# A chunked linear-attention and expert kernel on one core: scaling of group 0 read from the SBUF table, and a new order of all steps

## The chip, the core and the metric

The kernel runs on one core of a Trainium2 chip. Its engines work at the same time, each through its own instructions strictly in the order in which they were written: TensorE (PE in the profile, with PEld for its weight loads), VectorE (DVE), ScalarE (ACT), GpSimd (POOL) and SyncE (SP), which here only issues transfers. An instruction that waits holds up everything behind it on its engine. The metric is the device time of one execution in microseconds (us); lower is better.

## The reference

The first part is a linear attention with decay, for 4 batches, 8 heads, 768 time steps and head size 48. Its output `y`, as a matrix `x` of 3072 tokens by 384, goes through a two-layer block with a smooth ReLU between the layers.

```python
for t in range(S):
    cur = np.einsum('bhd,bhe->bhde', u[None] * kt, vt)
    y[:, :, t] = np.einsum('bhd,bhde->bhe', rt, state + cur)
    state = w[None, :, :, None] * state + np.einsum('bhd,bhe->bhde', kt, vt)
h = x @ w_in                      # 384 -> 2048
g = np.where(h >= 1, h, np.where(h <= -1, 0, (h + 1) ** 2 / 4))
out = g @ w_out                   # 2048 -> 384
```

Inputs and output are float32; the kernel computes its matrix products in bfloat16.

## The kernel before

The 768 steps are cut into 6 chunks of 128, and the 4 batches into 2 pairs; a pair's chunk is a *group*, so there are 12 groups, 0 to 11, of two units (batches) each. Groups 2c and 2c+1 are chunk c. A unit n has 128 tokens, one per partition. Inside a chunk the decay is taken out by scaling R up with w to the power t-64 (table Wup) and K down with its inverse (table Wdn).

Steps of a group g, by their names in the code; a suffix `.0` or `.1` means one unit alone:

- `LR`, `LK`, `LV` (line 252) load R, K and V on SP's queue, 384 KB each or 192 KB for a unit; `WI0` to `WI2` (line 243) and `WO0`, `WO1` (line 246) load the two weight matrices on GpSimd's queue, as bfloat16. `WI0` serves quarter 0 of the hidden layer, `WI1` quarter 1, `WI2` quarters 2 and 3.
- `Rs`, `Ks`, `KU`, `RKU` (line 271) are the products R·Wup, K·Wdn, K·u, R·K·u. `us` (line 293) sums the last over a head, `V` casts V to bfloat16 on ScalarE, `B` (line 302) is V times that sum.
- Rs and Ks have to stand transposed. Groups 0 and 1 and 2 do that on TensorE (`TR`, `TK`, `T`, line 319) and copy it out of PSUM (`cR`, `cK`, `c`); from group 3 on it is a DMA transpose on SP's queue (`RT`, `KT`, line 307).
- `A` (line 359; `AA` for both units) are the 128x128 products of K and R by head; `AT` (lines 368, 373) masks them on VectorE; `Y` (lines 421, 427) multiplies by V and by the state; `y` or `yg` (lines 435, 439) adds B. `Sp`, `Tm`, `decayg`, `sbf` carry the state on.
- The tokens are transposed to xT, by TensorE (`X`, `xc`) for the first groups and by a DMA transpose on SP's queue (`xcg`, line 456) from group 3 on.
- `m g.q` (line 464) is quarter q of the first layer: 12 matmuls of 256 columns into PSUM (`hp`). ScalarE squares the clamped value (`r`, lines 472 and 475; `s`, lines 482 and 484), VectorE ends it (`g`, line 487). `M g.jq` (line 499) is unit j and quarter q of the second layer, 4 matmuls of 384 columns into `op`. `og` or `o` copies it to SBUF, `stg` or `st` (lines 518, 515) stores it.
- `Z n` (line 526) is n matmuls on a zero tile, whose result nobody reads.

The order of all of this is one written-out list, `ORDER`; a loop at the end of the function calls the steps word by word, so each engine's and each queue's own order follows from the list. `=V`, `=A`, `=G` choose VectorE, ScalarE or GpSimd, and the digits behind a slash choose PSUM banks. Tiles come from pools with a fixed number of buffers (`SLOTS`), and a step that takes a buffer waits until the last reader of the old tile is done: for output tiles `o` that is the landing of the store.

In the preamble the logarithm of w is broadcast to all partitions by a matmul with ones (`bw`, line 206, tile `lwp`), and ScalarE takes exponentials of it: into SBUF (`WupS`, `WdnS`, lines 221 and 224), and into two PSUM banks (`Wup`, `Wdn`, lines 214 and 218, tiles `up_t` and `dn_t`), which only the `Rs` and `Ks` of group 0 read:

```python
t = flat(Wup) if g else tiles["up_t"]
```

Of the kernel before, what the change touches and what calls it, by code (L numbers as in the profile page):

```python
# [34 lines left out]
M1.01 AA3/13 AT6 X4/0 xc4=A M1.02 X5/0 xc5=A M1.03 og1=A LK5 AT7 Y6/1 m2.0/0 sbf3=A us3 Rs4=G RT4 Sp4/2 Sp5 Tmg2
r2.0=A s2.0=A B3=G Y7 yg3 xcg3 m2.1/3 r2.1=A m2.3/2 LV4 m2.2/1 Ks4=G KT4 g2.0 M2.00/0 M2.10 s2.1=A g2.1 M2.01 M2.11
LV6 r2.2=V m3.1/3 stg0 KU4=G RKU4=G LK6 LR6 r2.3=A s2.3=A s2.2=A decayg2=G g2.3 r3.1 m3.0/2 g2.2 M2.02 M2.03 Sp6/1 Sp7
us4 s3.1=A KU5=G M2.12 Ks5=G r3.0 g3.1 M2.13 s3.0=A KT5 Tmg3 og2=A Rs5=G m3.2/3 g3.0 LV5 V4 AA4/01 AT8 sbfg2=A
decayg3=G m3.3/2 RT5 AT9 B4=G M3.00/0 stg1 r3.2 s3.2=A M3.01 Y8/1 Y9 RKU5=G r3.3 g3.2 yg4 xcg4 s3.3=A V6 M3.10 M3.02
g3.3 KU6=G V5 sbfg3=A M3.11 LK10 stg2 us5 M3.12 M3.03 LR7 AA5/21 AT10 M3.13 Rs6=G og3=A m4.0/3 AT11 B5=G r4.0 LK7  # L40
m4.1/2 s4.0=A Y10/0 Y11 m4.2/1 r4.1 s4.1=A yg5 Ks6=G xcg5 RKU6=G m4.3/0 g4.0 RT6 M4.00/3 M4.10 r4.2 s4.2=A g4.1 Rs7=G
M4.11 Sp8/2 Sp9 KT6 M4.01 g4.2 LV7 LR8 M4.02 m5.1/1 LR9 r4.3 Tmg4 s4.3=A g4.3 decayg4=G us6 B6=G r5.1 KU7=G AA6/02
AT12 M4.03 LK8 sbfg4=A AT13 M4.12 M4.13 m5.0/0 s5.1=A RT7 g5.1 Ks7=G og4=A Y12/2 Y13 m5.2/1 r5.0 s5.0=A m5.3/3 yg6
xcg6 g5.0 RKU7=G Sp10/2 Sp11 r5.2 s5.2=A M5.00/0 M5.10 Ks8=G KT7 Tmg5 M5.11 LK9 decayg5=G g5.2 M5.01 M5.02 us7 m6.1/2
r5.3 s5.3=A g5.3 stg3 V7 LR11 B7=G r6.1 AA7/13 AT14 M5.12 KU8=G KT8 sbfg5=A s6.1=A M5.13 AT15 Rs8=G M5.03 og5=A m6.0/1
g6.1 LV8 r6.0 KU9=G RT8 s6.0=A Rs9=G Y14/3 Y15 Sp12/0 yg7 m6.2/2 m6.3/3 Sp13 xcg7 r6.2 stg4 g6.0 M6.00/1 s6.2=A Tmg6
decayg6=G r6.3 RT9 g6.2 M6.10 RKU8=G LR10 M6.11 Ks9=G M6.01 s6.3=A g6.3 stg5 M6.12 m7.1/0 AA8/32 M6.02 V8 r7.1 AT17
s7.1=A M6.13 KT9 M6.03 AT16 m7.0/2 sbfg6=A Sp14/3 Sp15 LV10 KU10=G us8 B8=G og6=A stg6 g7.1 r7.0 m7.2/1 s7.0=A Tmg7
LV9 Rs11=G g7.0 Y16/0 Y17 decayg7=G m7.3/3 yg8 r7.2 s7.2=A M7.00/2 xcg8 M7.10 Ks10=G r7.3 g7.2 s7.3=A g7.3 M7.11 M7.01
M7.02 V10 AA9/01 AT18 RT11 RKU9=G V9 M7.12 AT19 KT10 sbfg7=A M7.13 RKU10=G LK11 m8.0/3 Rs10=G M7.03 us9 r8.0 us10  # L50
og7=V s8.0=A g8.0 B9=G m8.1/1 r8.1 Y18/0 Y19 RT10 B10=G s8.1=A yg9 m8.2/2 r8.2 KU11=G xcg9 m8.3/3 s8.2=A g8.1 M8.00/0
LV11 M8.10 r8.3 M8.01 Sp16/1 g8.2 Sp17 Tmg8 M8.11 M8.12 stg7 m9.0/2 s8.3=A decayg8=G g8.3 AA10/31 AT21 M8.13 r9.0
M8.02 AT20 s9.0=A M8.03 m9.1/1 V11 sbfg8=A Y20/3 Y21 g9.0 Ks11=G og8=A yg10 xcg10 m9.2/0 r9.1 KT11 s9.1=A M9.00/3 r9.2
s9.2=A g9.1 m9.3/2 RKU11=G stg8 g9.2 M9.10 M9.11 r9.3 Sp18/1 Sp19 Tmg9 s9.3=A M9.01 M9.02 g9.3 decayg9=G us11 m10.0/0
r10.0 B11=G AA11/12 M9.12 M9.13 AT23 s10.0=A M9.03 sbfg9=A AT22 og9=V m10.1/2 stg9 Y22/1 Y23 g10.0 m10.2/3 r10.1
M10.00/0 s10.1=A r10.2 yg11 xcg11 g10.1 M10.10 m10.3/1 s10.2=A g10.2 r10.3 s10.3=A M10.01 M10.11 m11.1/2 M10.12 M10.02
g10.3 r11.1 m11.0/3 s11.1=A g11.1 M10.13 m11.2/1 r11.0 m11.3/2 s11.0=A r11.2 s11.2=A g11.0 M10.03 M11.10/3 og10=V
M11.11 r11.3 stg10 g11.2 M11.00/0 M11.01 M11.02 s11.3=A g11.3 M11.12 M11.13 M11.03 o11.1=A st11.1 o11.0=A st11.0
# [15 lines left out]
def kernel(  # L74
# [193 lines left out]
    def product(e, out, a, b, g, j):  # L268
        j0, j1 = by_unit(g, j)
        part = lambda x: x.rearrange("p (b h) d -> p b h d", b=UNITS)[:, j0:j1]  # L270
        engines[e].tensor_mul(part(out)[:, :, :, :D], part(a), rep(b, j1 - j0) if len(b.shape) == 3 and b.shape[1] == H else part(b))  # L271
# [295 lines left out]
```

## Time and profile before

| | |
|---|---|
| Median of 3 runs | 178.05 us (178.02 to 178.56) |
| The profiled execution's own time | 177.88 us |
| Its span, first to last instruction | 176.1 us |
| TensorE busy | 163.8 us, 93% of the span |
| VectorE, ScalarE, GpSimd busy | 131.0, 129.3, 114.9 us |
| Moved by DMA | 28.78 MB in 105,703 packets, of which 100,946 are under 512 bytes |

The span leaves out 1.78 us of the execution's time that lie ahead of its first and behind its last profiled instruction. The shares of busy time are means over a load-heavy first part, a long middle, and a tail; they don't say what ends a wait in any one of them. R, K and V are read in rows of 48 floats, 192 bytes, hence the small packets. `q1` is the transfer queue that SP issues to, `q0` that of GpSimd.

### The profile page before, as it was taken

How to read it: one execution, taken by the hardware profiler on the slowest of the kernel's cores; microseconds unless marked ns; L12 is line 12 of the kernel's file. 1: busy time of each engine (PE TensorE's matmuls, PEld its weight loads, DVE VectorE, ACT ScalarE, POOL GpSimd, SP SyncE). 2: the span in 40 equal slices, each digit the busy share in tenths (PEclk: the TensorE clock that was granted, in tenths of full speed). 3: DMA queues.
4: the chain of work that ended last, by engine and by line, in shares of the span. 5: the costliest groups of instructions: out<-in, count | busy, mean ns of one | idle time of the engine just before them, and what ended most of it. 6: DMA issues, size and time to landing. Idle time of an engine off the chain costs nothing.

```text
span 176.1 us, 3979 instructions
## 1 busy us (share of the span) xinstructions
PE 163.8 (93%) x1638; PEld 129.0 (73%) x1638; DVE 131.0 (74%) x149; ACT 129.3 (73%) x150; POOL 114.9 (65%) x83
## 2 busy tenths in 40 slices
...
GB/s 113 196 183 189 202 184 190 207 204 195 160 187 161 177 262 153 240 266 163 174 204 168 179 254 176 217 263 231 183 111 178 45 48 149 4 134 2 2 90 92
DMA packets 105703, 28.78 MB, mean 163 GB/s; under 512 B 100946, under 2 KB 104788, under 8 KB 105684
## 3 DMA queue, kind: packets, MB, share of 16 engines
...
q0 software_dynamic: 1744, 3.15, 9.8%
q8 instruction: 13, 0.21, 0.6%
...
q10 hardware_dynamic: 4, 0.00, 0.0%
HBM read 20.45 MB, written 4.72 MB: 143 GB/s over the span
## 4 chain that ended last, share of the span: by engine, by line
PE 51%; DMA 20%; SPq 15%; ACT 4%; DVE 4%; issue 2%; POOL 1%; ACTq 0%; POOLq 0%
PE hp L464 25%; PE op L499 20%; SPq L252 14%; DMA Ri<-in_r_dram 8%; DMA out_dram<-o 8%; DMA RT<-Rs 2%; DVE g L487 2%; DMA xT<-y 2%; PE A L359 2%; ACT pt L475 2%; PE Y L427 2%; PE Y L421 1%; ACT sq L484 1%; PE Sp L394 1%; POOL Rs L271 1%
## 5 line engine op out<-in xcount | busy, mean ns | idle before, releaser
L487 DVE SCALAR_TENSOR_TENSOR g<-sq,hp 128x1024 bf16<-128x1024 bf16 x48 | 58.4, 1218 | 17.1 <-ACT sq L484 16.8
L464 PE MATMUL hp<-xT,w_in 128*128 128x256 bf16 x576 | 68.8, 273 | 1.0 <-DMA xT<-y 0.8
L499 PE MATMUL op<-w_out,g 128*128 128x384 bf16 x384 | 68.5, 326 | 0.2 <-DVE g L487 0.2
L464 PEld LDWEIGHTS <-w_in 128*128 128x128 bf16 x576 | 61.9, 114 | 4.5 <-DMA xT<-y 1.4
L475 ACT ACTIVATE pt<-hp 128x1024 f32<-128x1024 f32 x46 | 46.9, 1019 | 19.1 <-PE hp L464 19.1
L499 PEld LDWEIGHTS <-g 128*128 128x128 bf16 x384 | 35.9, 98 | 22.4 <-DVE g L487 1.2
L484 ACT ACTIVATE sq<-pt 128x1024 bf16<-128x1024 f32 x46 | 48.7, 1058 | 1.4
L368 DVE TENSOR_TENSOR AT<-A,umask 128x1024 bf16<-128x1024 f32 x20 | 23.6, 1220 | 8.2 <-PE A L359 8.0
L271 POOL TENSOR_TENSOR Rs<-Ri,Wup 128x768 bf16<-128x768 f32 (+1 forms) x11 | 19.4, 1760 | 9.7 <-DMA Ri<-in_r_dram 9.7
L271 POOL TENSOR_TENSOR KU<-Ki,u_sb 128x768 f32<-128x768 f32 (+1 forms) x13 | 21.2, 1635 | 4.7 <-ACT u_sb L111 4.7
L271 POOL TENSOR_TENSOR RKU<-Ri,KU 128x768 f32<-128x768 f32 (+1 forms) x13 | 21.2, 1638 | 1.9 <-DVE KU L271 1.7
L405 POOL TENSOR_TENSOR state<-Tm,wCm 128x768 f32<-128x768 f32 x8 | 14.6, 1831 | 11.7 <-DVE Tm L402 11.7
L302 POOL TENSOR_TENSOR V<-Vb,diag 128x768 f32<-128x768 bf16 (+1 forms) x13 | 17.2, 1330 | 5.6 <-ACT Vb L111 4.5
L271 POOL TENSOR_TENSOR Ks<-Ki,Wdn 128x768 bf16<-128x768 f32 (+1 forms) x10 | 17.9, 1786 | 2.2 <-DMA Ki<-in_k_dram 2.1
L439 DVE TENSOR_TENSOR y<-Y,V 128x768 bf16<-128x768 f32 x10 | 9.6, 956 | 5.7 <-POOL RKU L271 2.4
L293 DVE TENSOR_REDUCE diag<-RKU 128x16 f32<-128x768 f32 (+1 forms) x14 | 11.6, 831 | 0.6 <-POOL RKU L271 0.6
L111 ACT COPY o<-op 128x768 f32<-128x768 f32 (+1 forms) x10 | 7.4, 737 | 6.3 <-PE op L499 3.3
L111 ACT CAST Vb<-Vi 128x768 bf16<-128x768 f32 (+1 forms) x14 | 10.2, 736 | 1.5 <-DMA Vi<-in_v_dram 1.5
L427 PE MATMUL Y<-Vb,AT 128*128 128x48 bf16 x192 | 10.5, 185 | 0.6 <-DVE state L398 0.6
L427 PEld LDWEIGHTS <-AT 128*128 128x128 bf16 x192 | 9.3, 97 | 1.4 <-issue 0.8
L402 DVE TENSOR_TENSOR Tm<-Sp,state 128x768 f32<-128x768 f32 x8 | 7.6, 955 | 1.5 <-PE Sp L394 1.4
L111 ACT CAST state_bf<-state 128x768 bf16<-128x768 f32 (+1 forms) x12 | 8.5, 720 | 0.0
...
## 6 DMA issues: line engine op xcount, KB each, us to landing
...
w_out<-in_moe_w_out_dram POOLq DMA_DIRECT2D x2, 768.0 KB, 10.2
...
```

What stands on the lines that cost most here:

```text
L111: nc.scalar.copy(out, in_) if e == "A" else engines[e].tensor_copy(out, in_)
L252: nc.sync.dma_start(out=t[:, j0 * H : j1 * H, :], in_=source(x, g, j0, j1))
L271: engines[e].tensor_mul(part(out)[:, :, :, :D], part(a), rep(b, j1 - j0) if len(b.shape) == 3 and b.shape[1] == H else part(b))
L302: engines[e].tensor_mul(t[:, hs, :], tiles["V", g][:, hs, :], tiles["diag", g][:, hs].unsqueeze(2).to_broadcast([P, n, D]))
L368: nc.vector.tensor_mul(t.rearrange("p i n t -> p (i n) t"), tiles["A", n].rearrange("p i (n t) -> p (i n) t", t=P), umask.unsqueeze(1).to_ ...
L405: engines[e].tensor_mul(states[g % BP], tiles["Tm", g], flat(wCm).unsqueeze(1).to_broadcast([P, UNITS, DM]))
L427: nc.tensor.matmul(Y[:, h * D : (h + 1) * D], AT[:, i, p, :], V[:, j * H + h, :], start=(c == 0), stop=True, skip_group_check=True,)
L464: nc.tensor.matmul(hp[:, f, :], w_in_sb[wi][:, i, wo * FG * P + f : (wo + 1) * FG * P : FG], tiles["xT", g][:, :, i, :], start=(i == 0), s ...
L475: nc.scalar.activation(t, tiles["hp", g, q], AF.Relu, bias=0.5, scale=0.5)
L484: nc.scalar.activation(t, p, AF.Square)
L487: nc.vector.scalar_tensor_tensor(out=make("g", ("g", g, q), [P, FG, TOK], BF16), in0=tiles["sq", g, q], scalar=1.0, in1=tiles["hp", g, q], ...
L499: nc.tensor.matmul(tiles[key][:, k, :DO], tiles["g", g, q][:, f, j * P : (j + 1) * P], w_out_sb[wi][:, wo, f * DO : (f + 1) * DO], start=( ...
```

## The change

Four things are changed.

1. The step `Wup` isn't in the list any more, so there is no PSUM table `up_t`; `Rs` of group 0 reads the SBUF table. (`Wdn` and its PSUM table stay, and `Ks` of group 0 still reads it.) All three steps `Rs0.0`, `Rs0.1`, `Rs1.0` run on VectorE.
2. The whole list is laid out anew: other positions, PSUM banks and, for some steps, other engines. `KU` of groups 0 and 3 and of unit 1.1 and `RKU` of group 1 go to VectorE, `RKU0.1`, `Ks1.1` and `Rs1.1` to GpSimd; the list keeps one step of each kind and unit.
3. There are 97 idle matmuls in the list where there were 56; those ahead of `bw` have 48 columns, the others 128.
4. Output tiles `o` have three buffers instead of two.

The diff, with the list cut to the lines that matter below:

```diff
 ORDER = """
-Zs/0 LK0.0 LR0.0 LK0.1 LR0.1 LR1.0 LR1.1 ln Z19 bw/2 WupS bu/1 Wdn/0 Ks0.1=V Wup/1 uS=A KU0.1=G Ks0.0=V Z5 TK0/3
-Rs0.0=V TR0/1 cK0=V Rs0.1=V TK1/0 cK1=A RKU0.1=V LV0.0 LV0.1 KU0.0=V RKU0.0=G WdnS us0.1 cR0=A Z14 A0/23 us0.0 AT0.0
-TR1/0 cR1=A Z4 A1/01 Rs1.1=V WI0 WI1 LK1.0 LK1.1 V0.0 wq/2 wE B0.0=G Rs1.0=G LV1.0 LV1.1 AT1.0 AT0.1 Z4 Y0/2 WI2 TR3/0
-LK2.0 AT1.1 Ks1.0=G cR3=A Ks1.1=V Z6 TK3/1 cK3=V V0.1 B0.1=G LR2.0 LR2.1 V1.0 y0 TR2/3 cR2=V LK2.1 Z2 A3/01 AT3.0 X0/2
-xc0=V KU1.1=G Y1/3 y1 KU1.0=G RKU1.0=G TK2/0 cK2=V Z2 X1/2 AT3.1 A2/30 AT2.1 wC=A Sp1/1 Tm1 xc1=A m0.0/0 r0.0=A s0.0=A
-m0.1/1 r0.1=A LK3 us1.0 AT2.0 RKU1.1=G us1.1 Sp2/0 Tm2 LR3 Y2/0 V1.1 Sp3/1 s0.1=A B1.0=V Y3/3 y2 X2/2 xc2=A g0.0
-m0.2/0 r0.2=A B1.1=G y3 X3/0 Sp0/2 g0.1 s0.2=A m0.3/1 r0.3=A s0.3=A Tm3 Tm0 xc3=V m1.2/3 m1.0/2 g0.2 WO0 WO1 Rs2=G
...
+Zs/1 LR0.0 LK0.0 LK0.1 ln Z44 bw/2 LR0.1 LR1.0 Wdn/0 bu/1 LV1.0 WupS LV0.0 Ks0.0=V Rs0.0=V uS=A KU0.0=V LV0.1 TK0/3
+cK0=A Ks0.1=V WdnS RKU0.0=G Z8 TR0/3 cR0=A WI0 KU0.1=V Rs0.1=V LK1.0 LK1.1 Z8 A0/12 TK1/0 WI1 TR1/3 AT0.0 cK1=A us0.0
+RKU0.1=G cR1=A V0.1 Z8 A1/13 LR1.1 V0.0 Rs1.0=V AT0.1 B0.0=G AT1.1 Z13 TR2/2 Y0/0 us0.1 wq/3 AT1.0 B0.1=G LV1.1 y0
+Y1/1 wE wC=V cR2=A Ks1.0=G Z2 X0/3 xc0=A y1 Z10 X1/0 KU1.0=G xc1=A TK2/1 cK2=A Z4 m0.0/0 WI2 RKU1.0=V V1.0 us1.0 LK2.0
+Sp1/3 A2/12 r0.0=A Tm1 m0.1/1 KU1.1=V LK2.1 s0.0=A AT2.0 Rs1.1=G Ks1.1=G g0.0 TR3/0 cR3=A AT2.1 r0.1=A TK3/0 B1.0=V
+LR2.0 Y2/3 Sp2/2 cK3=A y2 V1.1 RKU1.1=V A3/10 X2/3 us1.1 xc2=A AT3.1 s0.1=A B1.1=G Sp0/3 AT3.0 Sp3/0 WO0 m0.3/0 LR2.1
+g0.1 WO1 LR3 Y3/1 Tm2 m0.2/1 r0.3=A y3 Tm3 KU2=G LK3 s0.3=A Tm0 Ks2=G r0.2=A X3/1 xc3=V g0.3 m1.1/2 s0.2=A m1.0/3
+LV2.0 r1.1=V g0.2 RKU2=G m1.2/0 s1.1=A m1.3/1 Rs2=G g1.1 r1.2=A s1.2=A M0.00/2 r1.3=V M0.01 r1.0=A s1.3=A M0.10 g1.2
+M0.11 us2 T5/0 s1.0=A M0.12 g1.3 M0.13 c5=A LV2.1 M0.02 g1.0 sbf1=A A5/1 Rs3=G T4/0 AT5 M1.00/3 c4=A LV3 M1.10 sbf3=A
+Ks3=V M1.01 M1.11 A4/1 KU3=V KT3 M1.02 V2 AT4 RT3 M1.12 sbf0=A B2=G Sp4/0 Y4/1 LR4 Y5 Sp5 M0.03 RKU3=G yg2 LK4 M1.03
+og0=A Tmg2 X4/1 LK5 M1.13 xc4=A us3 sbf2=A decayg2=G X5/0 AA3/21 xc5=A m2.0/0 V3 AT6 LV5 og1=A B3=G AT7 m2.1/2 r2.0=A
...
-SLOTS = {..., "g": 13, "o": 2}
+SLOTS = {..., "g": 13, "o": 3}
...
     def do_Rs(e, b, g, j=None):
-        t = flat(Wup) if g else tiles["up_t"]
+        t = tiles["up_t"] if g == 0 and "up_t" in tiles else flat(Wup)
...
     def do_Ks(e, b, g, j=None):
-        t = flat(Wdn) if g else tiles["dn_t"]
+        t = tiles["dn_t"] if g == 0 and "dn_t" in tiles else flat(Wdn)
...
     def do_Z(e, b, n):
+        cols = P if "lwp" in tiles else D
         for i in range(n):
-            nc.tensor.matmul(tiles["z"][:, 0, :P], idle[:, :P], idle[:, :P], start=True, stop=True)
+            nc.tensor.matmul(tiles["z"][:, 0, :cols], idle[:, :P], idle[:, :cols], start=True, stop=True)
```

Further down both lists go through the groups in the same way, m, M, AA and Y of one group beside those of the next. What stands on TensorE's side of the list between a transfer's issue and the step that reads it differs:

| issue to reader | old list | new list |
|---|---|---|
| `xcg3` to `m3.1` | 3 m, 4 M | 1 m, 3 M |
| `RT5` to `AA5` | 7 M, 2 Y | 5 M, 2 Y |
| `xcg5` to `m5.1` | 1 m, 5 M, 2 Sp | 4 M |
| `RT8` to `AA8` | 3 m, 5 M, 2 Y, 2 Sp | 1 m, 5 M, 1 Sp |

Ahead of `M0.00`, counted from `m0.0`, the old list has 8 m, 2 Y, 3 Sp and 2 X on TensorE, the new one 8 m, 2 A, 2 Y, 4 Sp, 2 X, one `TR` and one `TK`; between `M0.00` and `AA3` it is 14 M, 2 T, 2 A, 2 Y in the old one and 16 M, 2 T, 2 A, 2 Y, 2 Sp, 2 X in the new one. The last output steps are `o11.1` and `o11.0`, on VectorE and ScalarE in the new list, both on ScalarE in the old one.

More of the change, by code (lines that the diff above doesn't have):

```diff
@@ L30 @@
-m0.1/1 r0.1=A LK3 us1.0 AT2.0 RKU1.1=G us1.1 Sp2/0 Tm2 LR3 Y2/0 V1.1 Sp3/1 s0.1=A B1.0=V Y3/3 y2 X2/2 xc2=A g0.0
-m0.2/0 r0.2=A B1.1=G y3 X3/0 Sp0/2 g0.1 s0.2=A m0.3/1 r0.3=A s0.3=A Tm3 Tm0 xc3=V m1.2/3 m1.0/2 g0.2 WO0 WO1 Rs2=G
-Ks2=G m1.1/0 r1.2=V g0.3 m1.3/1 KU2=G RKU2=G s1.2=A g1.2 LV2.0 LV2.1 LV3 M0.00/3 M0.10 M0.01 r1.0=A s1.0=A g1.0 r1.3=A
-s1.3=A M0.11 g1.3 M1.00/2 sbf1=A sbf0=A M1.10 Rs3=G M0.12 M0.13 T4/1 r1.1=A s1.1=A M0.02 M0.03 Ks3=V KT3 KU3=G c4=A
-T5/1 c5=A g1.1 us2 V2 B2=G A4/0 AT4 M1.11 RT3 LR4 LK4 A5/1 AT5 og0=A LR5 M1.12 M1.13 Y4/0 Y5 yg2 sbf2=A V3 RKU3=G
@@ L35 @@
[L35 to L58, printed above, removed]
+Zs/1 LR0.0 LK0.0 LK0.1 ln Z44 bw/2 LR0.1 LR1.0 Wdn/0 bu/1 LV1.0 WupS LV0.0 Ks0.0=V Rs0.0=V uS=A KU0.0=V LV0.1 TK0/3
```

25 lines of the change are left out of this document (24 added, 1 removed).

## The prediction

> **What bounds the kernel now.** I read the page first, then the chain of waits, then TensorE's timeline and its waits, then the transfer queues by windows.
>
> ```profile
> span 176.1 us, 3979 instructions
> PE 163.8 (93%) x1638; PEld 129.0 (73%) x1638; DVE 131.0 (74%) x149; ACT 129.3 (73%) x150; POOL 114.9 (65%) x83
> ```
>
> ```profile
> 25.58 14.41 DMA Ri<-in_r_dram
> ...
> 42.59 4.36 DMA RT<-Rs
> ...
> 47.09 0.62 PE A L359 x16
> ...
> 51.22 0.34 PE Sp L394 x8
> ...
> 60.53 4.72 DMA out_dram<-o
> ...
> 157.99 1.30 PE op L499 x8
> ...
> 163.86 2.62 PE hp L464 x24
> ...
> 168.15 4.52 DMA out_dram<-o
> ...
> 172.77 0.48 ACT o L111
> ```
>
> These are pieces of the chain that ended last. Up to 47 us it is SP's queue and the transfers behind it (R of group 3, then its transpose); from there it is nearly all TensorE. One m costs 1.31 us, one M 0.65, an AA 0.6 (so an A 0.3), a Sp 0.17.
>
> ```profile
> 19.90 2.78 PE L464 MATMUL hp<-xT,w_in 128*128 128x256 bf16 x24
> ...
> 24.89 0.33 PE L394 MATMUL Sp<-Vb,Ks 128*128 128x96 bf16 x4 [1.03 <-ACT Vb L111]
> ...
> 34.34 1.95 PE L499 MATMUL op<-w_out,g 128*128 128x384 bf16 x11
> ...
> 66.18 0.62 PE L359 MATMUL A<-RT,KT 48*128 48x128 bf16 x16 [0.83 <-ACT o L111]
> ...
> 68.07 1.46 PE L499 MATMUL op<-w_out,g 128*128 128x384 bf16 x8
> 69.37 0.21 PE L421 MATMUL Y<-state_bf,RT 128*128 128x96 bf16 x1
> ...
> 70.12 3.62 PE L499 MATMUL op<-w_out,g 128*128 128x384 bf16 x20
> ...
> 74.44 0.62 PE L359 MATMUL A<-RT,KT 48*128 48x128 bf16 x16 [0.69 <-DMA RT<-Rs]
> ...
> 166.32 6.01 PE L499 MATMUL op<-w_out,g 128*128 128x384 bf16 x36
> ```
>
> This is TensorE's timeline, with what ended its idle time in brackets. The first hp matmul starts at 19.90, the first op matmul at 34.34, the last ends at 166.32 + 6.01 = 172.33. Two Y take 70.12 - 69.37 = 0.75. So TensorE's own work from the first hp on is 48 x 1.31 + 96 x 0.65 = 125.3 for m and M, and about 18.7 for the rest (9 AA 5.4, 22 Y 7.9, 19 Sp 3.2, some transposes and two A 2.2): 144.0. The stretch is 172.33 - 19.90 = 152.4, so 8.4 us are lost. By stage: up to `M0.00` 14.44 - 11.8 = 2.6; from there to `AA3` at 47.09, 12.75 - 11.4 = 1.35; behind it 125.24 - 120.8 = 4.4. The time is the sum of four terms: the start of the first hp, the work behind it, what is lost, and a tail of 176.1 - 172.3 = 3.8.
>
> ```profile
> q1 hardware_dynamic: 10382, 1.96, 135.5%
> q0 software_dynamic: 1, 0.00, 0.2%
> ...
> q0 software_dynamic: 1189, 1.56, 84.3%
> q1 hardware_dynamic: 2577, 0.49, 31.0%
> ...
> q0 software_dynamic: 535, 1.55, 89.9%
> q1 hardware_dynamic: 1276, 0.24, 16.9%
> ```
>
> These are packets and MB of the two queues: SP's queue q1 alone from 2.8 to 13.0 us; both from 13.0 to 23.5, while w_in comes in; both from 28.4 to 37.5, while w_out does. The sum is 0.19 to 0.20 MB/us in each, a ceiling, but while weights flow q1 has only 0.047 and then 0.026 MB/us of it. Up to the landing of R of group 3 (25.58 + 14.41 = 40.0), ten inputs of 0.393 MB and 3.15 MB of weights have come, 7.1 MB in 37.2 us: the early part is set by bytes.
>
> **The named part: no PSUM table for R.**
>
> ```profile
> 6.13 1.02 DVE L271 TENSOR_TENSOR Ks<-Ki,dn_t 128x384 bf16<-128x384 f32 x2 [3.21 <-ACT dn_t L218]
> ...
> 6.02 0.56 ACT L214 ACTIVATE up_t<-lwp,up_col 128x384 f32<-128x384 f32 x1
> ...
> 7.07 0.55 DVE L271 TENSOR_TENSOR Rs<-Ri,up_t 128x384 bf16<-128x384 f32 x1
> ...
> 11.85 0.55 DVE L271 TENSOR_TENSOR Rs<-Ri,Wup 128x384 bf16<-128x384 f32 x1
> ```
>
> The timelines of VectorE and ScalarE have the product from the PSUM table and from the SBUF table at 0.55 us each: the operand's place costs nothing. ScalarE loses one exponential, 0.56. The new list puts `Wdn` first, so `Ks0.0` starts one exponential earlier, some 0.4 us, and `Rs0.0` finds `WupS` ready behind it. Were it slower instead, each of three 0.55 us products would grow; the nearest row, the same product on GpSimd at 1.0, bounds that at 1.4 us, and the two equal rows speak for 0.
>
> **When the first hp starts.**
>
> ```profile
> 7.07 1.00 POOL L271 TENSOR_TENSOR KU<-Ki,u_sb 128x384 f32<-128x384 f32 x1 [4.71 <-ACT u_sb L111]
> ...
> 10.69 1.70 POOL L243 DMA_DIRECT2D w_in<-in_moe_w_in_dram  x2
> ...
> 14.14 0.80 POOL L243 DMA_DIRECT2D w_in<-in_moe_w_in_dram  x1
> 14.97 1.39 POOL L271 TENSOR_TENSOR Ks<-Ki,Wdn 128x384 bf16<-128x384 f32 x1
> ...
> 25.69 1.48 POOL L246 DMA_DIRECT2D w_out<-in_moe_w_out_dram  x2
> 27.18 1.86 POOL L271 TENSOR_TENSOR Rs<-Ri,Wup 128x768 bf16<-128x768 f32 x1
> ```
>
> GpSimd's timeline. In the new list `KU0.0` is on VectorE, again behind u_sb (7.0), done at 7.55; `RKU0.0` on GpSimd follows until 8.55, and `WI0`, `WI1` are issued at 8.6, 2.1 us earlier. Their packets began 2.3 us behind the issue (10.69; one q0 packet lies ahead of 13.0), so now near 10.9. By then q1 has moved 8.1 x 0.193 = 1.56 MB, eight half loads of 0.197: K, R, V of group 0, R1.0 and V1.0 are in. The ninth, K1.0, still lacks 0.2 MB and gets q1's 0.047 MB/us: it lands near 15.5. The attention chain of group 0 itself, walked by rows (`Y0` 12.4, `y0` 13.3, `X0` 13.9, `y1` 14.4, `X1` 15.0, copy until 15.9), is ready earlier. But `TK2` stands ahead of `m0.0` on TensorE, and it needs `Ks1.0`, 1.39 us on GpSimd: 15.5 + 1.4 + a transpose and four idle matmuls 0.6 gives **17.5** for the first hp. Lower bound, if K1.0 were in before the weights, 16.4 (the copy of `X1`, then the same 0.6); upper bound, if q1 stands still until both weight parts are through (10.9 + 0.786/0.149 = 16.2, then 1 us for the load), 19.2.
>
> That is 2.4 us earlier, but 1.3 us of work that used to lie ahead of `m0.0` (two A, TR, TK, Sp) now lie behind: 145.3 instead of 144.0.
>
> The Trainium skill, DMA: Bandwidth & Descriptors, section Queues, rings and completion order, says that a DMA engine goes round its queues packet by packet. With 1 KB weight packets against 192 bytes, K1.0 would get 0.03 MB/us, land near 16.5 and set the first hp at 18.5, and as the same microsecond runs on through `WI2`, the sum would be 177.0; the measured 2577 packets against 1189 say that q1 gets more than one for one.
>
> **From there to `M0.00`.** `WI2` moves behind `Ks1.0` and `KU1.0` (15.5 + 1.4 + 1.0 = 18.0), 3.9 us later than the 14.14 of before; packets from 20.3, 0.786 MB at 0.15 to 0.18: in at 25.1. `m0.3` waits for it, where unhindered it would come at 17.5 + 4.8 = 22.3. Behind it stand 6 m, Y and X, 8.3 us, so `M0.00` at 33.4; VectorE, with `g` of 1.22 and `r1.1`, `r1.3` also on it, holds `m1.3` back by 0.6. I take **34.0** (33 to 35), against 34.34: most of the early lead is paid back to w_in, since the bytes haven't changed.
>
> **To `AA3`.** R and K of group 3 land by 40 as before, being the same bytes. `Ks3`, on VectorE behind `AT5`, is done near 41.8, and KT3 and RT3 go out after it, landing near 47.5 by the 4.36 of the chain. TensorE has 13.4 us of work in front of `AA3` now: 34.0 + 13.4 = 47.4. So **47.5**, later than 47.09, but with 118.8 us of work left instead of 120.8. The lead there is 120.8 + 47.09 - 118.8 - 47.5 = 1.6 us.
>
> **Behind `AA3`.**
>
> ```profile
> DMA to landing us min/median/max: 2.7/4.8/6.7
> ...
> DMA to landing us min/median/max: 2.8/4.8/6.6
> ...
> DMA to landing us min/median/max: 2.8/2.8/4.1
> ```
>
> ```profile
> 69.51 2.28 SPq L307 DMA_TRANSPOSE RT<-Rs  x1
> ```
>
> Issue to landing of the transposes KT, RT and xT, and SP's issue of `RT5`. The stall of 0.83 (1.0 in all) at 66.18 was `og2` waiting for the store that left at 60.53 to free an `o` buffer; with three buffers it goes. But the list leaves less work between issue and reader: `RT5` to `AA5` 4.0 us instead of 5.3, `xcg5` to `m5.1` 2.6 instead of 4.9, `xcg3` to `m3.1` 3.3 instead of 6.6, `RT8` to `AA8` 4.7 instead of 8.3. SP issued `RT5` 1.4 us behind its place in the list, which is ahead of `M3.00` (68.07), and I take the same lag for the others; against medians of 4.8 and 2.8 that lacks up to 2.2 at RT5, 1.6 at xT5, 0.9 at xT3, 1.5 at RT8. Each stall pushes TensorE back and so eases the next one; I take somewhat over half, 3.5, and 0.8 for small ones: 4.3, as before. GpSimd has one `KU` less there, at nothing on the path.
>
> **The tail.** `o11.0` waited from 172.33 for the store of `og10` (168.15 + 4.52 = 172.67) and started at 172.77. The third buffer frees it: 0.4 us.
>
> **The sum.** 47.5 + 118.8 + 4.3 = 170.6 for the last matmul (172.33 before), tail 3.4: span 174.0. With the 1.78 us between span and execution (177.88 - 176.1) that is 175.8; the median of the runs lies 0.17 above that execution, so **176.0**.
>
> **Rivals.**
>
> *The early lead stays.* If K1.0 and `WI2` don't hold TensorE up more than V1.1 did before (2.6 and 1.35 lost), the end is 16.4 + 145.3 + 7.4 (8.4 less the `o` stall) = 169.1, and the time 174.4. For it: `V1.1`, whose cast ended the 1.03 stall at 24.89, now lands ahead of `WI2`. Against it: the ceiling in MB/us.
>
> *Nothing comes of it.* `AA3` waits for RT3 until 49, because `Ks3` and `KU3` are now queued on VectorE between `AT5` and `AT4`, and the late stalls stay: 1.5 us more, 177.5.
>
> *R of group 2 starves (slower).* `T5` needs `Rs2`, which stands behind `RKU2` on GpSimd, and both need R2.1. By bytes R2.1 is in at 2.8 + (16 x 0.197 + 1.57)/0.193 = 27.3; w_out's packets begin about 27.5 in the new list. If w_out is first, R2.1 lands only at its end (27.5 + 9.1 = 36.6), `RKU2` and `Rs2` (1.86 each) end at 40.3, and `T5`, due at 34.0 + 2.6 = 36.6, holds TensorE for 3.7: 179.7. It decides from R2.1 landing later than 33. In the old kernel `Rs2` ran at 27.18, ahead of w_out.
>
> *The transposes are late one after another (slower).* If the four stalls come at full length and with the longest landings, 6.6 and 4.1, rather than medians, another 3 to 4 us: 179.5.
>
> That removing the PSUM table does nothing by itself is no rival but what the rows say; the sum doesn't rest on it.
>
> **Chances.** Forecast 0.43 (its own range 174.9 to 177.2), lead stays 0.15, nothing 0.18, starving 0.12, late transposes 0.10, anything else slower 0.02. A measurement tells 0.3%, 0.53 us, from no change. Faster: 0.43 + 0.15 and a quarter of the nothing case, less a little of the forecast's upper edge: 0.60. Same: 0.14. Slower: 0.26. The range leaves out the far ends of the slower cases and the best of the lead: 173.6 to 179.4.
>
> **What would show it.** Right: first hp between 16.4 and 19, just behind `TK2`; TensorE waiting for w_in or hp ahead of `m0.3`; `M0.00` within 1 us of 34; `AA3` with X4, X5 and all M1 done ahead of it; no wait of A on `o`; waits of A on RT or of hp on xT between 60 and 115 us. Wrong: `M0.00` ahead of 32.5 (the ceiling on bytes was misjudged), a wait at the transposes of `T5` (starving), or over 6 us lost behind `AA3`.

## The result, and the profile after

The changed kernel takes 180.73 us, the median of 18 executions (178.36 to 183.24), against 178.08 (176.84 to 179.87) for the kernel before on the same chip. The ratio is 1.011, with a 95% interval of 1.008 to 1.014: slower by 1.1%. A ratio here leaves out executions more than 1.5% above the fastest of their kernel, on either side, so it can lie below the quotient of two medians. The prediction was 176.0 with a range of 173.6 to 179.4: wrong, on the other side. The profiled execution of after took 180.69 us.

The page of the changed kernel: its span, TensorE's row, and the granted clock in 40 slices of 4.5 us.

```profile
span 178.9 us, 4053 instructions
PE 165.8 (93%) x1679; PEld 131.1 (73%) x1679; DVE 136.6 (76%) x152; ACT 128.6 (72%) x149; POOL 111.0 (62%) x80
...
PEclk9999987999999999999999996999999999999999
```

The span grew by 2.8 us. By the profile's windows the granted clock was at half twice, from 25.2 to 28.6 and from 107.1 to 110.5 us, and both times TensorE had m steps to run. In the kernel before it was at half once, from 13.1 to 16.5 us, ahead of any m.

TensorE's timeline of after, at the marks that the prediction used:

```profile
17.78 0.92 PE L464 MATMUL hp<-xT,w_in 128*128 128x256 bf16 x7
...
36.32 0.98 PE L499 MATMUL op<-w_out,g 128*128 128x384 bf16 x5
...
50.10 0.62 PE L359 MATMUL A<-RT,KT 48*128 48x128 bf16 x16
...
73.66 0.62 PE L359 MATMUL A<-RT,KT 48*128 48x128 bf16 x16 [0.84 <-DMA RT<-Rs]
...
106.63 4.45 PE L464 MATMUL hp<-xT,w_in 128*128 128x256 bf16 x24 [2.08 <-DVE o L111]
110.91 0.51 PE L394 MATMUL Sp<-Vb,Ks 128*128 128x96 bf16 x8
...
170.12 5.36 PE L499 MATMUL op<-w_out,g 128*128 128x384 bf16 x32
```

| mark on TensorE, us | before | predicted | after |
|---|---|---|---|
| first hp | 19.90 | 17.5 | 17.78 |
| `M0.00` | 34.34 | 34.0 | 36.32 |
| `AA3` | 47.09 | 47.5 | 50.10 |
| last matmul ends | 172.33 | 170.6 | 175.48 |
| tail | 3.8 | 3.4 | 3.4 |

So two stretches hold 4.3 of the 4.9 us by which the last matmul comes too late: from the first hp to `M0.00` 18.5 us instead of 16.5, and behind `AA3` 125.4 instead of 123.1.

Ahead of the first stretch there is a wait. TensorE's, VectorE's and GpSimd's timelines of after, between 13.8 and 17.1 us:

```profile
14.39 0.34 PE L449 MATMUL X<-ident,y 128*128 128x128 bf16 x3
14.57 0.72 PE L527 MATMUL z<-idle 128*128 128x128 bf16 x10
16.87 0.34 PE L449 MATMUL X<-ident,y 128*128 128x128 bf16 x3 [1.58 <-DVE y L435]
```

```profile
13.80 0.54 DVE L435 TENSOR_TENSOR y<-Y,V 128x384 bf16<-128x384 f32 x1
14.29 1.93 DVE L111 COPY wCm<-w_col 48x192 f32<-48x192 f32 x2
16.25 0.56 DVE L435 TENSOR_TENSOR y<-Y,V 128x384 bf16<-128x384 f32 x1
```

```profile
14.14 1.00 POOL L271 TENSOR_TENSOR Ks<-Ki,Wdn 128x384 bf16<-128x384 f32 x1
15.09 1.01 POOL L271 TENSOR_TENSOR KU<-Ki,u_sb 128x384 f32<-128x384 f32 x1
```

`y1` stands on VectorE behind the two copies of `wC`, which the new list moved there from ScalarE. They took 0.96 us each. `X1`, and `m0.0` behind it, wait for `y1`. K1.0 was no limit: `Ks1.0` began at 14.14.

The stretch behind `AA3` has one stall that was in no step of the prediction. VectorE's timeline and the chain of waits of after:

```profile
105.62 0.96 DVE L111 COPY o<-op 128x768 f32<-128x768 f32 x1 [2.78 <-DMA out_dram<-o]
```

```profile
99.06 6.46 DMA out_dram<-o
106.63 4.45 PE hp L464 x24
```

`og5` needs the `o` buffer of `og2`, the third before it. SP issued the store `stg2` only at 99.06 us, since it stands far back in the list, and it landed 6.46 us later. `og5` waited 2.78 us on VectorE; `m6.3` takes the PSUM pair that `og5` frees and waited 2.1. Half a microsecond behind that gap the clock went to half, and `m6.3` and `m6.2` took 4.45 us for 24 matmuls, which take 2.62 at full clock (the prediction's chain of before, at 163.86).

### The profile page after: what moved, and what is told of

It reads as the page before. It is cut to its first block, busy times and chain, and to the rows that moved or that the text cites. A ratio compares the mean times of both kernels' runs of the same rounds, so it can differ in the third digit from the quotient of the medians.

```text
span 178.9 us, 4053 instructions
## 1 busy us (share of the span) xinstructions
PE 165.8 (93%) x1679; PEld 131.1 (73%) x1679; DVE 136.6 (76%) x152; ACT 128.6 (72%) x149; POOL 111.0 (62%) x80
## 4 chain that ended last, share of the span: by engine, by line
PE 63%; DMA 13%; DVE 10%; SPq 4%; POOL 3%; ACT 3%; issue 3%; DVEq 0%; ACTq 0%; POOLq 0%
PE hp L464 28%; PE op L499 24%; DMA Ki<-in_k_dram 4%; DMA out_dram<-o 4%; DMA Vi<-in_v_dram 3%; DVE AT L373 2%; PE A L359 2%; DMA RT<-Rs 2%; PE Sp L394 2%; SPq L307 2%; SPq L252 1%; PE Y L427 1%; DVE y L435 1%; PE Y L421 1%; POOL Ks L271 1%
## 5 line engine op out<-in xcount | busy, mean ns | idle before, releaser
L464 PE MATMUL hp<-xT,w_in 128*128 128x256 bf16 x576 | 71.8, 280 | 3.2 <-DVE o L111 2.1
L464 PEld LDWEIGHTS <-w_in 128*128 128x128 bf16 x576 | 63.2, 116 | 8.0 <-issue 3.4
L475 ACT ACTIVATE pt<-hp 128x1024 f32<-128x1024 f32 x45 | 45.9, 1020 | 21.5 <-PE hp L464 21.3
L484 ACT ACTIVATE sq<-pt 128x1024 bf16<-128x1024 f32 x45 | 47.4, 1057 | 1.2
L271 POOL TENSOR_TENSOR RKU<-Ri,KU 128x768 f32<-128x768 f32 (+1 forms) x12 | 20.2, 1688 | 5.5 <-DVE KU L271 5.2
L271 POOL TENSOR_TENSOR Ks<-Ki,Wdn 128x768 bf16<-128x768 f32 (+1 forms) x11 | 18.4, 1677 | 0.4 <-DMA Ki<-in_k_dram 0.3
L271 POOL TENSOR_TENSOR KU<-Ki,u_sb 128x768 f32<-128x768 f32 (+1 forms) x10 | 17.5, 1751 | 0.0
L293 DVE TENSOR_REDUCE diag<-RKU 128x16 f32<-128x768 f32 (+1 forms) x14 | 11.6, 830 | 0.1
L111 ACT COPY o<-op 128x768 f32<-128x768 f32 (+1 forms) x8 | 6.0, 755 | 7.0 <-PE op L499 7.0
```

What stands on the lines that cost most here:

```text
L111: nc.scalar.copy(out, in_) if e == "A" else engines[e].tensor_copy(out, in_)
L293: nc.vector.tensor_reduce(d[:, hs], tiles["RKU", g][:, hs, :], AX.X, ALU.add)
L464: nc.tensor.matmul(hp[:, f, :], w_in_sb[wi][:, i, wo * FG * P + f : (wo + 1) * FG * P : FG], tiles["xT", g][:, :, i, :], start=(i == 0), s ...
L475: nc.scalar.activation(t, tiles["hp", g, q], AF.Relu, bias=0.5, scale=0.5)
L484: nc.scalar.activation(t, p, AF.Square)
```

## The experiments

Three theories. **A**: the loss has two places, the start held by other engines' queues (`wC` on VectorE first of all) and `og5` behind `stg2`, each made larger by the half clock that follows. **B**: the start alone, bound by the arrival of inputs and weights whatever the order. **C**: late transposes all over the new list. All kernels compute the whole output. The results, as ratios to the kernel before, whose median was 178.08 beside after and 178.34 to 178.68 in the other four groups of runs:

| kernel | median of all, us | ratio, 95% interval | executions in the ratio |
|---|---|---|---|
| after | 180.73 | 1.011 (1.008 to 1.014) | 12 of 18 |
| old_start | 178.43 | 1.002 (0.999 to 1.005) | 10 of 10 |
| new_start | 179.12 | 1.004 (1.000 to 1.007) | 10 of 10 |
| wc_act | 178.80 | 1.000 (0.997 to 1.003) | 10 of 10 |
| stg2_early | 179.25 | 0.998 (0.992 to 1.004) | 4 of 10 |
| both | 176.49 | 0.9915 (0.9875 to 0.9954) | 9 of 10 |
| warm | 176.91 | 0.9914 (0.9875 to 0.9953) | 8 of 10 |
| queue | 178.90 | 0.988 (0.979 to 0.997) | 2 of 10 |
| fill | 175.99 | 0.986 (0.982 to 0.990) | 5 of 6 |
| best | 176.81 | 0.989 (0.984 to 0.993) | 4 of 6 |
| fill_warm | 177.23 | 0.994 (0.991 to 0.997) | 11 of 11 |
| fill_wcv | 177.56 | 0.991 (0.987 to 0.995) | 7 of 9 |
| no_z | 179.73 | 1.008 (1.005 to 1.012) | 8 of 8 |
| no_table | 178.90 | 1.005 (1.002 to 1.009) | 10 of 10 |
| no_table_v | 178.62 | 1.0005 (0.9975 to 1.0035) | 11 of 12 |
| o3 | 179.11 | 1.002 (0.999 to 1.005) | 11 of 12 |

### Which half of the order: old_start and new_start

```
old_start:  old list up to m2.0 | new list behind it (PSUM pairs 1 and 3 exchanged), three o buffers
new_start:  new list up to m2.0 | old list behind it (the same exchange), three o buffers
```

> The old list up to the first hp step of group 2 (m2.0), then the new list's order for all steps that are left, PSUM banks 1 and 3 swapped so that they fit, three o buffers. Theory A (the loss sits in two places: a start that is slow on VectorE, and og5 behind the store of og2 near 105 us): the start is the old one (m2.0 near 49.7) and the rest loses what the new one lost, 6.4 us, of which 3.9 at og5: span near 177.9, ratio to the kernel before 1.010. Theory B (the start alone is at fault): ratio 1.00 or below. Theory C (transposes with less work ahead of their readers cost the time, all over the middle): as in A, 1.010, but without one large wait.

> The new list up to m2.0, then the old list's order for the rest, banks 1 and 3 swapped, three o buffers. Theory A: m2.0 near 50.7, 1 us later than before, and then the old losses of 4.2 less the 1.0 us of og2's wait: span 175.6 against 176.1, ratio 0.997. Theory B: all of the loss comes with the start: 1.011. Theory C: 0.995 to 1.00.

Neither half alone gives the 1.1%. Theory A's numbers, 1.010 and 0.997, are missed on both sides. In old_start's profile the stall at `m6.3` is 0.66 us, in after's 2.08; in new_start's, `m2.0` starts at 52.97, later than after's 50.73. Each half lies within 0.4% of before, and the new list as a whole does not. Theory B, the start alone, asked for 1.011 in new_start, which lies outside its interval. What each place costs is settled by the next runs.

### The two places: wc_act, stg2_early, both

```diff
 (wc_act)       Y1/1 wE -wC=V cR2=A ... TK2/1 cK2=A +wC=A Z4 m0.0/0
 (stg2_early)   xcg5 +stg2 s4.2=A ... M5.12 -stg2 V7
 (both)         the two edits together
```

> The changed kernel with the two copies wC on ScalarE behind cK2 instead of on VectorE ahead of y1. Theory A: y1 starts at 14.4 instead of 16.25, the first hp near 16.4 instead of 17.8, and about 1 us of that is left at the end: 179.7 against 180.7, ratio to the kernel before 1.005. Rival (bytes): the first hp comes as early, but M0.00 and AA3 stay where they are, since w_in and group 3 land when they did: ratio 1.011.

> The changed kernel with the store stg2 moved up in the list, from behind LR8 to right behind xcg5 (issue near 84 instead of 99 us). Theory A: og5 finds its buffer free, and the 2.2 us wait of m6.3 and the 1.7 us of half clock behind it go: 3.9 us less, span 175.0, ratio to the kernel before 0.993. Theory C: the transposes behind it are as late as they were, and the gain is below 1 us, ratio 1.007 or more. Theory B: no gain.

> The changed kernel with two edits: the wC copies on ScalarE behind cK2, and the store stg2 right behind xcg5. Theory A (two local places): the stall of 2.2 us at m6.3 goes, first hp at about 16.0, and the group-1 stalls stay as they are without wC on VectorE (M0.00 at about 36.0): span 176 to 177, ratio 0.990 to 0.998. Theory C (late transposes everywhere): what is gained at m6.3 shows again at AA5 and m6.1 (1 us or more each): ratio 0.998 to 1.004.

wc_act: ScalarE's and TensorE's timelines. On ScalarE the two copies take 0.71 together; `X1` starts at 15.12 and the first hp at 16.02, 1.76 us earlier than in after.

```profile
16.34 0.71 ACT L111 COPY wCm<-w_col 48x192 f32<-48x192 f32 x2
```

```profile
15.12 0.33 PE L449 MATMUL X<-ident,y 128*128 128x128 bf16 x3
...
16.02 1.47 PE L464 MATMUL hp<-xT,w_in 128*128 128x256 bf16 x12
...
24.61 2.76 PE L464 MATMUL hp<-xT,w_in 128*128 128x256 bf16 x12
...
27.51 2.61 PE L464 MATMUL hp<-xT,w_in 128*128 128x256 bf16 x12
```

stg2_early: `og5` on VectorE follows the instruction ahead of it without a wait, and `m6.3` has no stall.

```profile
102.88 1.21 DVE L368 TENSOR_TENSOR AT<-A,umask 128x1024 bf16<-128x1024 f32 x1
104.02 0.95 DVE L111 COPY o<-op 128x768 f32<-128x768 f32 x1
```

Each edit by itself takes about 1.1% and 1.3% off after, and neither interval meets that of after; stg2_early's ratio rests on four executions, and by the medians in the table its edit takes 1.0% off. Both together take 2.0% off: 0.9915 against 1.011. Theory C had 0.998 or more for `both`, and it is missed. That settles the result. Without these two the new list is 0.85% faster than the old one, 176.49 us, near the 176.0 of the prediction (by luck in good part, as the account of the prediction shows).

The clock part of A shows in two profiles with the same list up to 60 us. In wc_act the clock was down from 23.0 to 29.9, and `m0.3` and `m0.2` took 2.76 and 2.61 us (above). In `both` it was not, and TensorE's timeline reads:

```profile
24.52 1.47 PE L464 MATMUL hp<-xT,w_in 128*128 128x256 bf16 x12
25.83 0.36 PE L427 MATMUL Y<-Vb,AT 128*128 128x48 bf16 x8
26.08 1.47 PE L464 MATMUL hp<-xT,w_in 128*128 128x256 bf16 x12
27.39 0.33 PE L449 MATMUL X<-ident,y 128*128 128x128 bf16 x3
28.21 5.40 PE L464 MATMUL hp<-xT,w_in 128*128 128x256 bf16 x48 [0.49 <-DVE xT L111]
33.44 0.81 PE L499 MATMUL op<-w_out,g 128*128 128x384 bf16 x4
```

`M0.00` starts at 33.44 here, at 35.98 in wc_act: 6.8 us at half clock, two windows of 3.4, cost 2.5 us up to that mark. The executions of `both` show what is left of such a price at the end. The two with a mean clock of 1.000 took 175.6 and 175.9 us, the five between 0.987 and 0.990 (one window) 176.1 to 176.9, the two at 0.981 and 0.980 (two windows) 177.4 and 178.1. So one window goes with some 0.7 us and two with some 1.9; no edit sets the windows here, so that they cost this is argued and not tested.

### What the idle matmuls and the half clock are worth: warm, no_z, fill_warm

```diff
 (warm, fill_warm)  both / fill, and
   +Zb/3 +Z3 TR3   +Z10 TK3   +Z4 Y2   +Zs/0 +Z9 Sp0   +Z4 Sp3     (Zb: z in a PSUM bank)
 (no_z)             both without any Z step
```

> The kernel both with 30 more idle matmuls, 128 wide, in the gaps of TensorE in group 1 (ahead of TR3, TK3, Y2, Sp0 and Sp3) and nothing else. Theory A, clock part: the half-clock windows near 23 to 30 us go, m0.3 and m0.2 take 1.3 us and not 2.5 each, M0.00 starts 1.5 to 2.5 us earlier than in both (at 33.5 to 34.5), ratio 0.008 to 0.014 below that of both. Theory B (the start is bound by the arrival of the inputs, or by VectorE's queue): M0.00 moves by less than 0.5 us and the ratio by less than 0.003.

> The kernel both without any idle matmul (97 of 128 columns left out; they write nothing that is read). If the idle matmuls of the changed kernel do keep the clock up (theory A, clock part): at least one half-clock window more in the first 30 us, M0.00 at 34.5 to 36 and not 33.4, ratio 0.004 to 0.014 above that of both. If they only stand in the way of other work: the same windows, and the ratio within 0.003 of that of both or below it.

> The kernel fill with the 30 idle matmuls of warm in the gaps of TensorE in group 1. In fill's profile a half-clock window at 23.0 to 26.4 made Y3 wait (0.9 us) and M0.00 start at 34.3, in both without a window at 33.4. If such a window costs what it costs at that place: M0.00 at 33.3 to 33.6, granted clock 1.00 in nearly all executions, ratio 0.003 to 0.006 below fill's. If the later arrival of w_out and the late transposes set the pace anyway (as warm against both says, 0.9914 against 0.9915): ratio within 0.003 of fill's.

no_z is 1.7% slower than `both` (1.0082 against 0.9915), about 3 us: that is what the idle matmuls of the new list are worth against none. `M0.00` starts at 36.10, 2.7 us later than in `both`. TensorE's timeline of no_z is slow at the first hp and ahead of it; in `both` the same `TR2` takes 0.39 and the first m 1.47.

```profile
12.28 0.59 PE L319 MATMUL TR<-ident,Rs 128*128 128x128 bf16 x4 [0.53 <-DVE AT L373]
...
17.20 2.71 PE L464 MATMUL hp<-xT,w_in 128*128 128x256 bf16 x12
```

The trace's first record of a full clock stands at 22.4 us in no_z, at 11.7 in `both`, 11.6 in after, 9.7 in before. The mean granted clock is 1.000 for no_z all the same: the half speed ahead of the first record isn't in it. So the expectation, a half-clock window more, has the right place, but the window is one that never began.

The 30 further idle matmuls did what they were put in for, and won nothing. With them the clock was 0.997 to 1.000 in every execution that the two ratios rest on, but warm has the ratio of `both` (0.9914 against 0.9915), and fill_warm is slower than fill, though measured beside another group of runs. By the executions of `both` above, a clock at 1.000 alone should have won something; warm's took 175.7 to 177.1 us, and the two of `both` at 1.000 took 175.6 and 175.9. So the 30 matmuls seem to cost about what they save. How they cost it wasn't tested; one profile shows a place. `M0.00` starts at 33.44 in fill_warm and at 34.34 in fill, and by `m5.0` the order is turned, 87.91 against 87.31: the transpose of xT for group 5 was issued at 79.54 in fill_warm and 80.53 in fill, but landed at 83.91 and 83.31, and TensorE waited 1.55 us for it in fill_warm. A lead of 0.9 us at the start was lost to a slower transfer. Of the clock part of A the mechanism is shown; the 0.8 to 1.4% that warm was to gain by it is refuted.

### The late transposes: fill, and o3

```diff
 (fill)  both, and
   M3.12 LR7 +M3.02 AA5/31 ... AT10 -M3.02 AT11
   g5.3 Rs9=G +M5.02 m6.1/1 ... AT15 -M5.02 AT14
   stg5 +M7.03 m8.0/3 LV10 AT18 -M7.03 r8.0
 (o3)    the kernel of before:   "o": 2   ->   "o": 3
```

> The kernel both with three steps moved on TensorE's queue alone: M3.02 ahead of AA5, M5.02 ahead of m6.1, M7.03 ahead of m8.0, all of them ready while AA5, m6.1 and m8.0 wait for a late transpose (1.1, 0.8 and 0.7 us in both). Theory C (the late transposes are a real loss of the new order, but one that order on TensorE alone can fill): 0.65 us each, together 1.5 to 2.0 us, ratio 0.008 to 0.011 below that of both. If something behind sets the pace (ScalarE's and VectorE's queues, the loads): the stalls show again elsewhere, and the ratio is within 0.004 of that of both.

> The kernel of before with three o buffers in place of two, nothing else. The prediction's terms: og2's wait for its buffer (1.0 us ahead of AA4) goes and the tail gets 0.4 us shorter: ratio 0.992, and AA4 shows no stall. Theory A holds that a buffer more only lets the stores be issued later without a wait; in the old list the stores stand close behind their copies, so no copy waits 2 us for one: ratio 0.992 to 1.000, no stall of over 1 us by an o copy.

TensorE's timelines at `AA5`, of `both` and of fill:

```profile
66.89 3.56 PE L499 MATMUL op<-w_out,g 128*128 128x384 bf16 x20
71.40 0.62 PE L359 MATMUL A<-RT,KT 48*128 48x128 bf16 x16 [0.95 <-DMA RT<-Rs]
```

```profile
67.62 4.06 PE L499 MATMUL op<-w_out,g 128*128 128x384 bf16 x24
71.61 0.62 PE L359 MATMUL A<-RT,KT 48*128 48x128 bf16 x16
```

The 24 op matmuls of fill cover the wait that stood behind 20. fill has the lowest ratio of all, 0.986 (0.982 to 0.990), 1.4% faster than before and 2.5% faster than after. Against `both` it is 0.6% faster, with intervals that overlap, so a gain over `both` isn't shown; the expectation was 0.8 to 1.1%.

o3 is the plainest test of a term of the prediction. The `o` wait at `AA4` went, as foreseen, but TensorE's timeline shows what came in its place:

```profile
65.30 0.62 PE L359 MATMUL A<-RT,KT 48*128 48x128 bf16 x16
...
74.77 0.62 PE L359 MATMUL A<-RT,KT 48*128 48x128 bf16 x16 [2.13 <-DMA RT<-Rs]
```

`AA5` waits 2.1 us for RT5, where it waited 0.7 before: RT5 landed at 74.6 us in o3 and at 74.3 in before, whatever TensorE had gained ahead of it. Behind that wait the clock was at half from 76.3 to 79.7 us. The tail got 0.4 us shorter, as foreseen. The buffer alone is worth nothing, 1.002 (0.999 to 1.005), not the 0.992 that the two terms made.

### The named part: no_table, no_table_v, fill_wcv

```diff
 (no_table)    the old list -Wup/1; Rs of group 0 reads the SBUF table; two o buffers
 (no_table_v)  no_table, -KU0.1=G, and Rs0.0=V +KU0.1=V TR0/1
 (fill_wcv)    fill, -wC=A behind cK2, and us1.0 +wC=V
```

> The named part by itself: the list of before, without the step that fills the PSUM table, so that both products Rs of group 0 read the SBUF table; two o buffers, the old order otherwise, its idle matmuls at 128 columns. All theories but one say that the table is worth nothing (both products took 0.55 us from either table on VectorE, and the step was over before anything waited for it): ratio to before 1.000, between 0.996 and 1.004, first hp within 0.5 us of 19.9. If the table itself were the loss, 1.01.

> The kernel no_table with one product moved: KU0.1 on VectorE behind Rs0.0, and not on GpSimd beside it. In no_table Rs0.0 took 1.26 us (7.07 to 8.33) with both operands in SBUF while GpSimd ran KU0.1 (6.92 to 7.91); in before, from the PSUM table and beside the same KU0.1, 0.55. Theory P (a VectorE product of two SBUF operands waits for a GpSimd product that runs beside it): Rs0.0 takes 0.55 us, TR0 starts at about 7.7 and not 8.4, TensorE gets its full clock near 10 us and not at 19.9, first hp 1.0 to 2.0 us earlier than no_table's 21.76. Theory Q (an SBUF table is itself slow at this place): Rs0.0 stays at 1.2 to 1.3 us and TR0 at 8.4.

> The kernel fill with the two wC copies back on VectorE, but behind us1.0 (near 17.3 us), where GpSimd runs nothing, and not between Y1 and y1. Theory P (the two copies took 0.96 us each in the changed kernel, since GpSimd ran Ks1.0 and KU1.0 beside them): 0.2 to 0.5 us each here. Theory Q (a copy of this form takes VectorE 0.96 us wherever it stands): 0.96 each again, and Tm1 and AT2.0 are 1.2 us later. Either way first hp stays at about 16.0, since y1 no longer stands behind them; ratio to before within 0.004 of that of fill under P, up to 0.005 above it under Q.

The table by itself costs about 0.5% in the old list (0.1 to 0.9%), where at most 0.4% was expected. VectorE's, GpSimd's and TensorE's timelines of no_table:

```profile
7.07 1.26 DVE L271 TENSOR_TENSOR Rs<-Ri,Wup 128x384 bf16<-128x384 f32 x1
```

```profile
6.92 0.99 POOL L271 TENSOR_TENSOR KU<-Ki,u_sb 128x384 f32<-128x384 f32 x1 [4.58 <-ACT u_sb L111]
```

```profile
8.38 0.61 PE L319 MATMUL TR<-ident,Rs 128*128 128x128 bf16 x4 [0.57 <-DVE Rs L271]
```

And VectorE's of no_table_v, where nothing runs on GpSimd at that time:

```profile
7.07 0.55 DVE L271 TENSOR_TENSOR Rs<-Ri,Wup 128x384 bf16<-128x384 f32 x1
```

The same product of the same operands takes 0.55 us alone and 1.26 beside a product on GpSimd. From PSUM, in the kernel before, it took 0.55 beside that very `KU0.1` (7.07 to 8.07 on GpSimd). In no_table TensorE idles for it, gets its full clock at 19.9 us and not at 9.7, and the first hp starts at 21.76; in no_table_v these are 10.6 (with the clock at half again from 14.0 to 20.9) and 20.29, and the ratio is 1.0005. The expected 10 us and 1 to 2 us hold. The two products are compared cleanly; the 0.5% is less firm, since the intervals of no_table and no_table_v overlap, and the clock is that of one execution each.

fill_wcv does the same for `wC`. VectorE's timeline:

```profile
17.21 0.51 DVE L111 COPY wCm<-w_col 48x192 f32<-48x192 f32 x2
```

Two copies in 0.51 us with GpSimd idle, against 1.93 with `Ks1.0` and `KU1.0` beside them. In after the first ended 0.1 us behind the end of `Ks1.0`, the second as closely behind `KU1.0`: VectorE was held until GpSimd was done. The first hp stayed at 16.1. The ratio, 0.991, is 0.005 above fill's with overlapping intervals, where at most 0.004 was expected under P. The time of the copies decides for P; a gain over ScalarE's 0.71 us doesn't show in the kernel's time.

The Trainium skill, SBUF — State Buffer, section Who interferes with whom, states this: a VectorE instruction with two SBUF inputs contends with a GpSimd instruction that reads SBUF, and a VectorE copy can do so too, while a reduction doesn't, nor, outside such copies, an instruction with at most one SBUF input; the one that comes second blocks. The traces agree: 1.26 and 0.96 us against 0.55 and 0.25, and 0.55 with a PSUM operand. `us0.0`, a reduction, took its usual 0.54 us at 10.28 in after with a GpSimd product beside it all the time.

### The order of group 1: queue and best

```diff
 (queue, from both)   AT2.0 +AT2.1 ... +Y2/3 +TK3/0 +y2 +g0.0 ... X2/3 xc2=A A3/10 ... m0.3/0 ahead of Sp3/0
                      RKU1.1=V -> =G   B1.0=V -> =G   WO0 ahead of B1.1
 (best, from fill)    AT2.0 +AT2.1 +B1.0=V ... +Y2/3 +y2 +g0.0 TK3/0 ... X2/3 xc2=A ... A3/10
                      RKU1.1=V -> =G
```

> The kernel both with the steps of group 1 from AT2.0 to y3 in another order and no idle matmul more: RKU1.1 and B1.0 on GpSimd, AT2.1 and y2 ahead of g0.0 on VectorE, Y2 ahead of TK3, X2 and xc2 ahead of A3, m0.3 ahead of Sp3, WO0 ahead of B1.1. Theory A, queue part: the waits ahead of Y2, Sp0 and Sp3 go (about 1.1 us), m0.3 starts 1.5 to 2 us earlier than in both, M0.00 1.5 to 3 us earlier, ratio 0.008 to 0.015 below that of both. Theory B: M0.00 moves by less than 0.5 us, since R2, K2 or the weights arrive too late for it, and the ratio by less than 0.003.

> The kernel fill with the steps of group 1 mended, and the stores and loads of the weights left where they are: AT2.1, B1.0 and y2 ahead of g0.0 on VectorE, RKU1.1 on GpSimd, Y2 ahead of TK3, X2 and xc2 ahead of A3. m0.3 at 24.0 to 24.4 (w_in2 lands at about 24.0), M0.00 at 32.8 to 33.4, M0.12 still behind w_out's second part: 0 to 0.6 us less than fill, ratio to before 0.978 to 0.988. If the rule of the run queue holds (whatever brings a weight or R2 later costs more than the queues give): T5 late, ratio above that of fill.

Nothing was won. best, at 0.989, lies between `both` and fill, and in its profile `M0.00` starts at 34.66, where 32.8 to 33.4 was expected. queue's executions lie far apart (174.94 to 180.60) and its ratio rests on two of them, so it settles nothing about group 1's order. Whether the waits there can be taken out stays open.

## Why the prediction was wrong, by its steps

**The named part.** "The operand's place costs nothing" rested on two rows of 0.55 us, and the one from SBUF had no GpSimd product beside it. The step fails: in no_table `Rs0.0` took 1.26 us, and the kernel 0.5% more. VectorE's timeline of before already held a row against it, with `w_in` being issued and `Ks1.0` run on GpSimd in the same time:

```profile
14.11 1.40 DVE L271 TENSOR_TENSOR Ks<-Ki,Wdn 128x384 bf16<-128x384 f32 x1
```

Its own bound, up to 1.4 us, would have held it. In the new list the three products came out at 0.56, 0.54 and 0.88 us; most of the price fell on `KU0.1`, 1.12 us beside `RKU0.0`, and on `wC`.

**When the first hp starts.** 17.5 was forecast, 17.78 measured, and the reason was wrong. K1.0 was in by 14.1, not 15.5 or later. What held `m0.0` was `wC` on VectorE, a move that the prediction never priced; wc_act starts at 16.02, ahead of the 16.4 of the lower bound.

**From there to `M0.00`.** The mark came at 36.32, 2.3 us later than forecast. The step put the loss on w_in2, landing at 25.1; that landed at 23.8 and nobody waited for it. What TensorE waited for were copies and masks of group 1, and then `m0.3` ran at half clock. TensorE's timeline of after:

```profile
22.08 0.38 PE L319 MATMUL TK<-ident,Ks 128*128 128x128 bf16 x4 [0.67 <-ACT TT L111]
...
23.32 0.35 PE L427 MATMUL Y<-Vb,AT 128*128 128x48 bf16 x7 [0.83 <-DVE AT L373]
...
25.35 0.48 PE L394 MATMUL Sp<-Vb,Ks 128*128 128x96 bf16 x4 [0.57 <-ACT xT L111]
...
26.37 2.58 PE L464 MATMUL hp<-xT,w_in 128*128 128x256 bf16 x12
```

With 0.28 at `X2` and 0.26 at `Sp3` the waits make 2.6 us. Half clock behind a thin stretch was in no step, though the granted clock of before already showed such a window.

**To `AA3`.** Right as a difference: 13.5 forecast, 13.8 measured. The rival of a starving R2 did not come.

**Behind `AA3`.** 4.3 us of loss were forecast, 6.6 measured (125.4 less 118.8). That is over 6, one of the prediction's own signs of being wrong. RT5 was late, by 0.84, xT3 by 0.27, and the `o` wait at 66 us was gone; xT5 and RT8 weren't late. The term that failed is the third buffer: the step followed it to `og2` and to the tail (3.4, right) and not to the next wait that it makes, `og5` behind a store that the new list issues at 99 us. In after's profile it took 2.1 us of waiting and 1.8 of half clock (4.45 less 2.62), 3.9 of the 6.6; stg2_early shows it to be worth 1.0 to 1.3%. The other 2.7 us are less than the 4.3, so the term of the late transposes was too large and hid part of the miss.

**What was not counted at all.** The idle matmuls, worth 1.7% against none by no_z; what the 97 gain over the 56 of the old list wasn't measured. With `wC` and `stg2` mended the kernel comes out at 176.49, near the sum of 176.0, but that is luck. In the profile of `both` the first hp, `M0.00`, `AA3` and the last matmul's end stand at 16.04, 33.44, 48.01 and 170.47. Against the forecast the four stages are off by -1.5, +0.9, +1.1 and -0.6 us, which cancel. Neither of the two slower rivals came: `T5` waited for nothing, and of four late transposes only RT5 cost more than 0.5 us.
